# Dense layers without GpSimd: sums and low parts on VectorE, relu and squares on ScalarE, PSUM banks in pairs

## The chip, the cores and the metric

The kernel is one program on one core of a Trainium2 chip. The core has a matrix engine (TensorE, PE in the profile), a vector engine (VectorE, DVE), a scalar engine (ScalarE, ACT), a slower general engine (GpSimd, POOL) and SyncE (SP), which issues transfers. Each engine runs its own instructions in order and waits on semaphores for the others. The metric is the device time of one execution in microseconds (us).

## The reference, cut to what matters

Three layers follow each other over 8 batches of 576 tokens with 512 features.

```
x = linear attention of q, k, v                  # 8 heads of 64, out: 8 x 576 x 512
xk, xr = mu*x + (1-mu)*x_prev                    # two mixes with the token before
k = max(xk @ w_k, 0);  v = (k*k) @ w_v           # 512 -> 1024 -> 512
x2 = sigmoid(xr @ w_r) * v                       # 512 -> 512
gate = sigmoid(causal convolution of x2, 5 taps per feature)
out = (gate * (x2 @ w_val)) @ w_out              # two more 512 x 512
```

All matrices are fp32. The weights arrive as 64-bit bits and are turned into fp32 on the chip.

## The kernel before, in words

The first third of the time is attention (lines up to L760); beside it GpSimd, VectorE and ScalarE convert the weights. `moe()` then does the dense layers, one batch at a time: a loop of nine turns (`it`), in which turn `it` runs `prep` (the two mixes), `st_k`, `st_r` and `st_v` of batch `it`, and `conv`, `st_val` and `st_out` of batch `it-1`. On TensorE the stages of a turn stand in the order k, r, val, v, out. `x`, its mixes and `x2` have features on the partitions and 576 tokens (two halves of 288, `TB`) along the free dimension.

Each fp32 operand is split into a high part (a ScalarE copy to fp32r) and a low part (the operand less its high part); `product` adds three matmuls, high-high, high-low and low-high, into one PSUM bank. A matmul has 128x288 outputs. `st_k` and `st_v` use a scheme with seven products instead of eight: `combos` forms sums of the operand's quarters and `operand` splits them, into four buffers of the page `ops` (turn by turn); a product has 24 matmuls. `st_r`, `st_val` and `st_out` (`gemm`) have 96 plain matmuls each. That makes 7 x 24 x 2 + 3 x 96 = 624 matmuls in a full turn.

In the version before, the quarter sums of `combos` and many low parts (those not in `fast`) run on GpSimd through `pool_tt` (L395), in pieces of 288 columns; the rest of the low parts are VectorE's (`less`, L312). Results leave PSUM bank by bank, 288 columns at a time: copies by ScalarE, sums by VectorE (`dve`, L787), and relu with square in one VectorE instruction (`relu2`, L794). `fma` (L790) is VectorE's multiply by a per-feature factor and add, in `prep` and `conv`.

The pages are SBUF areas with changing contents. `xb` holds the batch's x with a zero column in front (its memset stands at L877, the load beside it in `prep`) and, later in the turn, x2 split for `st_val`. Weights of r, val, v and out come from DRAM in units of 1 MB into three buffers `u` (the first of v into `xf`); SyncE issues these loads and that of x in one queue.

`Order` plans all this when the program is built: each piece of work is an entry with an engine, a planned duration (`t_dve`, `t_act`, `t_pool`, `t_mm`), what it reads and writes, and a due time (`when`). `run` repeatedly takes the entry that could start first and appends its instructions to its engine, so that the durations in the plan decide the order on each engine. `Banks` gives out the eight PSUM banks. The waits between engines are then put in from the addresses that instructions touch.

Of the kernel before, what the change touches and what calls it, by code (L numbers as in the profile page):

```python
# [50 lines left out]
class Buf:  # L51


    def __init__(self, tag, make):
        self.tag, self.make, self.tile, self.users = tag, make, None, []
# [5 lines left out]
class Banks:  # L61


    def __init__(self, tiles, most):
        self.most, self.held, self.tiles = most, [], tiles

    def when(self, tasks, new):

        live, found, out = dict.fromkeys(self.most, 0), [], set(range(len(self.tiles)))
        for b in self.held:  # L70
            out.discard(b.place)
            ends = [tasks[u]["end"] for u in b.users]
            if None in ends:
                live[b.tag] += 1
            else:
                found.append((max(ends) + SEM, b.place, b))
# [4 lines left out]
        if any(b.tag in LAST for b in new) and sum(live[x] for x in LAST) >= len(self.tiles):  # L81
            return None
        found = sorted([(0.0, i, None) for i in out] + found, key=lambda f: f[:2])
        return found[:len(new)] if len(found) >= len(new) else None

    def take(self, found, new):
        for (_, place, old), b in zip(found, new):
            if old is not None:
                self.held.remove(old)
            b.place, b.tile = place, self.tiles[place]  # L90
            self.held.append(b)
# [12 lines left out]
class Order:  # L104
# [29 lines left out]
    def run(self):  # L134
# [10 lines left out]
        def ready(t):  # L145
            at = 0.0
            for d in t["deps"]:
# [3 lines left out]
                at = max(at, d["end"] + (SAME if d["eng"] == t["eng"] else SEM))  # L151
# [95 lines left out]
def build(ctx, tc, qt, kt, vv, wphi, mu, wk, wr, wv, wval, cw, wout, out):  # L247
# [5 lines left out]
    PSB = {"pj": 4, "qp": 2, "nm": 3, "kv": 2, "tb": 2, "mk": 8, "mo": 8}  # L253
# [24 lines left out]
    banks = [psum.tile([128, 512], F32, tag=f"b{i}", name=f"b{i}", bufs=1) for i in range(8)]  # L278
# [133 lines left out]
    def combine(quarters, n, emit):  # L412
# [16 lines left out]
        emit(1, s2, [t2])  # L429
        emit(2, a12, [t12])  # L430
# [53 lines left out]
    mut = const.tile([128, 2, 4], F32, name="mut")  # L484
    cwr = const.tile([128, 20, 2], I32, name="cwr")
# [257 lines left out]
    def moe():  # L743
# [41 lines left out]

        def dve(n, out, x, y, op, r, w):
            add("DVE", t_dve(n), lambda: tt(out=out(), in0=x(), in1=y(), op=op), r=r, w=w)  # L787

        def fma(n, out, x, scalar, y, r, w):
            add("DVE", t_dve(n) + 0.06, lambda: stt(out=out(), in0=x(), scalar=scalar(), in1=y(), op0=ALU.mult,  # L790
                                                    op1=ALU.add), r=r, w=w)

        def relu2(n, out, x, r, w):
            add("DVE", t_dve(n) + 0.06, lambda: stt(out=out(), in0=x(), scalar=0.0, in1=x(), op0=ALU.max,  # L794
                                                    op1=ALU.mult), r=r, w=w)

        def bank(o):
            return lambda: o[:, 0:TB]

        def product(o, stat, mov, first, last):  # L800

            k, n = 0, 3 * len(stat)
            for c, (wh, wl) in enumerate(stat):
                for a, b in ((wh, 0), (wh, 1), (wl, 0)):
                    mm(out=o[:, 0:TB], lhsT=a, rhs=mov[b][c], start=first and k == 0, stop=last and k == n - 1,  # L805
# [21 lines left out]
        def operand(x, fast):  # L827
# [3 lines left out]
            add("ACT", t_act(576), lambda: copy(h(F32R), x()), r=x.tok, w=h.tok)  # L831
# [6 lines left out]
        def combos(ops, qs, tmps, due, fast):  # L838

            each = list(enumerate(zip(qs, tmps)))  # L840

            def sub(p, i, out, x, y):
                due(p, i)
                pool_tt(576, out, x, y, ALU.subtract, tokens(x, y), out.tok)

            def op(p, k):
                for i, (q, tmp) in each:
                    due(p, i)
                    ops[p, i] = operand(tmp if k is None else q[k], p in fast)
# [3 lines left out]
            for i, (q, tmp) in each:  # L853
                sub(1 - 0.6, i, tmp, q[3], q[1])
                sub(1 - 0.4, i, q[1], q[1], q[0])
                sub(1 - 0.2, i, q[0], q[3], q[1])
            for p, k in enumerate((0, 2, 1, None, 3, 2), 1):
                op(p, k)
                if p == 2:
                    for i, (q, tmp) in each:  # L860
                        sub(2.2, i, q[2], q[0], q[2])
                yield

        def x2_at(it, m, h, n=TB):
            return At("x2", 2432 * (it % 2) + 608 * m + 32 + TB * h, n)

# [5 lines left out]
        def prep(it):  # L872
# [11 lines left out]
            for c in range(4):  # L884
                kh, cc = divmod(c, 2)
                when(it, -26 + 2.5 * c)
                dve(576, d[c], lambda c=c: x()[:, c, 1:577], lambda c=c: x()[:, c, 0:576], ALU.subtract,
                    x.tok + ["x0"], d[c].tok)
                fma(576, lambda kh=kh, cc=cc: view("xf", 1152 * kh, [128, 2, 2, 288])[:, :, cc],
# [275 lines left out]
```

## Time and profile before

| | us |
|---|---|
| median of 3 runs (1084.04 to 1088.51) | 1086.49 |
| profiled execution | 1086.6 |
| its span | 1084.8 |
| TensorE busy | 998.2 |
| VectorE busy | 891.2 |
| GpSimd busy | 686.1 |
| ScalarE busy | 495.0 |

The span is what the profile covers; 1.8 us of the profiled execution lie outside it. TensorE's instructions overlap (a weight load and the matmul before it, and each matmul with the next), so a busy TensorE need not be at its best rate; that rate is read as matmuls for each stretch of time. The chain of work that ended last is 50% TensorE, 29% VectorE and 11% GpSimd.

### The profile page before, as it was taken

How to read it: one execution, taken by the hardware profiler on the slowest of the kernel's cores; microseconds unless marked ns; L12 is line 12 of the kernel's file. 1: busy time of each engine (PE TensorE's matmuls, PEld its weight loads, DVE VectorE, ACT ScalarE, POOL GpSimd, SP SyncE). 2: the span in 40 equal slices, each digit the busy share in tenths (PEclk: the TensorE clock that was granted, in tenths of full speed). 3: DMA queues.
4: the chain of work that ended last, by engine and by line, in shares of the span. 5: the costliest groups of instructions: out<-in, count | busy, mean ns of one | idle time of the engine just before them, and what ended most of it. 6: DMA issues, size and time to landing. Idle time of an engine off the chain costs nothing.

```text
span 1084.8 us, 27608 instructions
## 1 busy us (share of the span) xinstructions
PE 998.2 (92%) x11456; PEld 957.2 (88%) x11456; DVE 891.2 (82%) x1328; ACT 495.0 (46%) x1031; POOL 686.1 (63%) x759
## 2 busy tenths in 40 slices
PE   8998898998988989998998899899889989988998
PEld 7888787887877988997998899899889989988998
DVE  6869686878878899789869959987995997799572
ACT  4676566766756343335342432523333252433342
POOL 1596887687745677486659548566864855686430
PEclk9999999999999998998999999899999989999999
DMA  7646567788844361483376157238516724841583
GB/s 207 192 145 190 162 207 236 235 273 252 264 148 143 134 239 40 140 303 111 117 267 209 40 190 268 95 117 282 194 40 206 276 72 138 291 164 53 181 276 123
DMA packets 93949, 195.86 MB, mean 181 GB/s; under 512 B 42496, under 2 KB 64384, under 8 KB 80512
## 3 DMA queue, kind: packets, MB, share of 16 engines
q1 hardware_dynamic: 84016, 184.00, 51.6%
q10 hardware_dynamic: 9808, 10.10, 2.7%
q8 instruction: 90, 1.47, 0.6%
q14 instruction: 35, 0.29, 0.1%
HBM read 161.57 MB, written 32.51 MB: 179 GB/s over the span
## 4 chain that ended last, share of the span: by engine, by line
PE 50%; DVE 29%; POOL 11%; issue 4%; ACT 3%; DMA 2%; SPq 1%; ACTq 0%; DVEq 0%; POOLq 0%
PE b L805 38%; DVE g L790 8%; PE b L649 4%; DVE ops L312 3%; DVE xb L790 3%; DVE x L787 3%; PE b L543 3%; DVE xf L790 2%; PE b L683 2%; DVE xb L787 2%; POOL xf L353 2%; DVE sp L787 2%; PE b L608 2%; POOL xb L395 1%; POOL xf L395 1%
## 5 line engine op out<-in xcount | busy, mean ns | idle before, releaser
L805 PE MATMUL b<-ops,wkt 128*128 128x288 f32 x1344 | 209.0, 318 | 38.2 <-DVE sp L787 15.4
L805 PEld LDWEIGHTS b<-ops,wkt 128*128 128x128 f32 x1344 | 198.7, 206 | 47.4 <-DVE sp L787 16.8
L805 PE MATMUL b<-y,u 128*128 128x288 f32 x1536 | 206.8, 295 | 1.7 <-DVE k L787 1.2
L805 PEld LDWEIGHTS b<-y,u 128*128 128x128 f32 x1536 | 204.4, 188 | 2.4 <-DVE k L787 1.4
L805 PE MATMUL b<-ops,u 128*128 128x288 f32 x1152 | 161.0, 297 | 8.7 <-POOL ops L395 5.3
L805 PEld LDWEIGHTS b<-ops,u 128*128 128x128 f32 x1152 | 154.7, 188 | 14.2 <-POOL ops L395 8.9
L790 DVE SCALAR_TENSOR_TENSOR g<-x,cwt,g 128x576 f32<-128x576 f32 x128 | 137.4, 1117 | 0.2
L395 POOL TENSOR_TENSOR ops<-xf,ops 128x288 fp32r<-128x288 f32 x84 | 91.4, 1109 | 54.6 <-ACT ops L309 47.7
L549 DVE TENSOR_REDUCE ot<-b 128x4 f32<-128x512 f32 (+1 forms) x160 | 94.3, 624 | 25.9 <-PE b L543 22.7
L309 ACT ACTIVATE ops<-k 128x576 fp32r<-128x576 f32 x96 | 66.1, 689 | 106.6 <-POOL k L395 59.2
L395 POOL TENSOR_TENSOR ops<-k,ops 128x288 fp32r<-128x288 f32 x56 | 54.5, 995 | 92.5 <-ACT ops L309 92.4
L312 DVE TENSOR_TENSOR ops<-k,ops 128x576 fp32r<-128x576 f32 x68 | 77.2, 1145 | 41.1 <-ACT ops L309 41.0
L395 POOL TENSOR_TENSOR k<-k 128x288 f32<-128x288 f32 x96 | 97.7, 1046 | 18.5 <-DVE ops L312 18.5
L805 PE MATMUL b<-xb,u 128*128 128x288 f32 x768 | 103.1, 295 | 0.0
L805 PEld LDWEIGHTS b<-xb,u 128*128 128x128 f32 x768 | 102.3, 188 | 0.0
L543 PE MATMUL b<-wph,ops 64*128 64x128 f32 x1152 | 80.6, 285 | 4.7 <-DVE k L551 1.2
L543 PEld LDWEIGHTS b<-wph,ops 64*128 64x128 f32 x1152 | 70.8, 191 | 12.9 <-issue 5.8
L794 DVE SCALAR_TENSOR_TENSOR k<-k 128x288 f32<-128x288 f32 x96 | 80.0, 852 | 2.0 <-POOL k L395 2.0
L683 PE MATMUL b<-g,y 128*64 128x65 f32 x2176 | 74.0, 224 | 6.2 <-ACT g L309 4.2
L683 PEld LDWEIGHTS b<-g,y 128*64 128x64 f32 x2176 | 68.1, 139 | 11.8 <-ACT g L309 4.8
L612 ACT ACTIVATE y<-b 128x512 f32<-128x512 f32 x128 | 68.8, 601 | 12.9 <-PE b L608 12.5
L395 POOL TENSOR_TENSOR xf<-xf 128x288 f32<-128x288 f32 (+1 forms) x62 | 67.5, 1112 | 5.2 <-DVE xf L364 5.1
(124 smaller groups left out, 1725.4 us busy)
## 6 DMA issues: line engine op xcount, KB each, us to landing
u<-ws SPq DMA_DIRECT2D x96, 1024.0 KB, 4.8
ws<-xb SPq DMA_DIRECT2D x24, 512.0 KB, 3.8
xs<-x SPq DMA_DIRECT2D x16, 576.0 KB, 4.5
xb<-xs SPq DMA_DIRECT2D x8, 1152.0 KB, 7.3
out<-ot ACTq DMA_DIRECT2D x64, 144.0 KB, 1.8
ops<-in_kt SPq DMA_DIRECT2D x15, 576.0 KB, 5.3
ops<-in_qt SPq DMA_DIRECT2D x15, 576.0 KB, 5.3
u<-in_vv SPq DMA_DIRECT2D x16, 512.0 KB, 5.5
```

The lines of the kernel that those rows point to most:

```text
L309: act(out=out, in_=x, func=AF.Copy)
L312: eng.tensor_tensor(out=out, in0=x, in1=hi.bitcast(F32), op=ALU.subtract)
L395: nc.gpsimd.tensor_tensor(out=o[:, c], in0=a[:, c], in1=b[:, c], op=op)
L543: mm(out=bs[ab][:, (at + i) * 128:(at + i + 1) * 128], lhsT=x[r, c:c + 128], rhs=wph[r], start=True, stop=True)
L549: add("DVE", t_dve(128 * n), lambda: nc.vector.tensor_reduce(out=m[:, 0:n, 0], in_=b3[:, 0:n], axis=AX.X, op=ALU.max, apply_absolute_value ...
L612: add("ACT", t_act(512), lambda half=half: act(out=e[:, ab, half, :], in_=b[:], func=AF.Exp, scale=-1.0 if half else 1.0), r=[b], w=[(e, a ...
L649: mm(out=b[y, o:o + 65], lhsT=lhs[:, y], rhs=vt[:, a:a + 65], start=(k == 0), stop=(c == 3), skip_group_check=True)
L683: mm(out=b[rows, at:at + 65], lhsT=lhs, rhs=a[:, o:o + 65], start=(k == 0), stop=(half == 1), skip_group_check=True)
L787: add("DVE", t_dve(n), lambda: tt(out=out(), in0=x(), in1=y(), op=op), r=r, w=w)
L790: add("DVE", t_dve(n) + 0.06, lambda: stt(out=out(), in0=x(), scalar=scalar(), in1=y(), op0=ALU.mult, op1=ALU.add), r=r, w=w)
L794: add("DVE", t_dve(n) + 0.06, lambda: stt(out=out(), in0=x(), scalar=0.0, in1=x(), op0=ALU.max, op1=ALU.mult), r=r, w=w)
L805: mm(out=o[:, 0:TB], lhsT=a, rhs=mov[b][c], start=first and k == 0, stop=last and k == n - 1, skip_group_check=True)
```

## The change

In `moe()` nothing runs on GpSimd any more. All low parts and all sums of quarters are VectorE's; those of `st_v` are single instructions over 1152 columns. Relu and square are two ScalarE instructions (`square`). The seven products are ordered so that running sums stay in PSUM (`PLAN`: product p adds into bank pair A, B or C, and only 0, 1 and 3 start afresh). PSUM is given out as four pairs of banks in the dense layers, and a result is read as 2 x 288 = 576 columns by one instruction. In `prep` the mix is a ScalarE scaling and one `fma` with 1-mu (`omm`) instead of a difference and an `fma`; the first tap of `conv` is a ScalarE scaling. The output leaves in 32 transfers of 288 KB instead of 64 of 144 KB. The planned durations become `d_time` and `a_time`, and an entry may follow another on TensorE without a planned gap. The diff, cut:

```
-    banks = [psum.tile([128, 512], F32, tag=f"b{i}", name=f"b{i}", bufs=1) for i in range(8)]
+    banks = [psum.tile([128, 2, 512], F32, tag=f"b{i}", name=f"b{i}", bufs=1) for i in range(4)]
...
-                at = max(at, d["end"] + (SAME if d["eng"] == t["eng"] else SEM))
+                at = max(at, d["end"] + (SEM if d["eng"] != t["eng"] else 0.0 if t["eng"] == "PE" else SAME))
...
+        def d_time(n):
+            return 0.15 + 0.00104 * n
+
+        def a_time(n):
+            return 0.13 + 0.00094 * n
...
-        def operand(x, fast):
+        def operand(x):
-            if fast:
-                add("DVE", t_dve(576), lambda: less(nc.vector, l(F32R), x(), h(F32R)), r=tokens(x, h), w=l.tok)
-            else:
-                pool_tt(576, lambda: l(F32R), x, h, ALU.subtract, tokens(x, h), l.tok)
+            add("DVE", d_time(576), lambda: less(nc.vector, l(F32R), x(), h(F32R)), r=tokens(x, h), w=l.tok)
...
-                pool_tt(576, out, x, y, ALU.subtract, tokens(x, y), out.tok)
+                dve(n, out, x, y, ALU.subtract, tokens(x, y), out.tok)
...
+                    acts(576, out, now, AF.Copy, x.tok + ["mut"], toks, scale=lambda r=r, c=c: mut[:, r, c:c + 1])
+                    fma(576, out, was, lambda r=r, c=c: omm[:, r, c:c + 1], out, x.tok + ["x0", "omm"], toks)
...
+        def square(it, t, x):
+            when(it, t)
+            acts(576, x, x, AF.Relu, [], x.tok)
+            acts(576, x, x, AF.Square, [], x.tok)
+
+        PLAN = ("A", "B", "A", "C", "A", "C", "A")
+        FRESH = (0, 1, 3)
...
+                    if p in (0, 2, 3, 4):
+                        d = (x11, None, x12, p5[m2], x22)[p]
+                        acts(576, d, b, AF.Copy, [o], d.tok)
+                        if p == 4:
+                            dve(576, x22, x22, p5[m2], ALU.add, p5[m2].tok, x22.tok)
+                            square(it, t + 4, x22)
+                    elif p == 6:
+                        acts(576, x21, b, AF.Relu, [o], x21.tok)
+                        acts(576, x21, x21, AF.Square, [], x21.tok)
                     else:
+                        d = x11 if p == 1 else x12
+                        dve(576, d, d, b, ALU.add, [o], d.tok)
+                        square(it, t + 4, d)
```

What the planner makes of it is seen in the order of the instructions. The first place is VectorE where `st_val` of a turn ends and `st_v` begins: `g` times the last results of val, the memset of the zero column of `xb` for the next batch, the low part of the last `y`, and low parts of v's operands (`ops` from `k`). Before:

```order
L787 TENSOR_TENSOR g<-g,b_80 128x288 [waits PE_49]
L787 TENSOR_TENSOR g<-g,b_84 128x288 [waits PE_49]
L877 MEMSET xb 128x4
L312 TENSOR_TENSOR y<-g,y 128x576 [waits Activation_49]
L312 TENSOR_TENSOR ops<-k_4936,ops 128x576 [waits Activation_49]
L787 TENSOR_TENSOR sp<-sp,b_86 128x288 [waits PE_49]
```

and now:

```order
L806 TENSOR_TENSOR g<-g,b_82 128x576 [waits PE_49]
L912 MEMSET xb 128x4 [waits DMAHW3_49]
L324 TENSOR_TENSOR y<-g,y 128x576 [waits Activation_49]
L324 TENSOR_TENSOR ops<-k_4934,ops 128x576 [waits Activation_49] x3
L806 TENSOR_TENSOR sp<-sp,b_83 128x576 [waits PE_49]
L324 TENSOR_TENSOR ops<-k_4934,ops 128x576 [waits Activation_49]
```

The memset stands at the same place, but now it waits for a transfer (DMAHW). The second place is SyncE's queue around that transfer, from the first unit of v (`xf`) to the load of x (`xb`). Before:

```order
L330 DMA xf<-ws 128x2048 [waits DVE_49,DMAHW2_49,Activation_49,Pool_49]
L330 DMA u_4938<-ws 128x2048 [waits DMAHW7_49,DMAHW3_49,PE_49]
L330 DMA u_4937<-ws 128x2048 [waits DMAHW4_49,PE_49]
L330 DMA u_4675<-ws 128x2048 [waits DMAHW5_49,DMAHW0_49,PE_49]
L330 DMA u_4938<-ws 128x2048 [waits DMAHW6_49,DMAHW3_49,PE_49]
L330 DMA xb<-xs_99 128x4x576 [waits DMAHW7_49,DMAHW1_49,DVE_49]
```

and now:

```order
L342 DMA xf<-ws 128x2048 [waits DVE_49]
L342 DMA u_4936<-ws 128x2048 [waits DMAHW1_49,PE_49]
L342 DMA u_4935<-ws 128x2048 [waits DMAHW3_49,DMAHW2_49,PE_49]
L342 DMA u_4673<-ws 128x2048 [waits DMAHW6_49,PE_49]
L342 DMA u_4936<-ws 128x2048 [waits DMAHW4_49,DMAHW1_49,PE_49]
L342 DMA xb<-xs_94 128x4x576 [waits DMAHW5_49,DVE_49]
```

The load of x stands at the same place, behind the unit whose buffer the last product of val frees. Before, the VectorE instruction that it waits for is the memset above; now it is an older one (a low part of `xb`), and the memset is the one that waits for the load. (The zero column and the loaded columns lie in one 4 x 577 area.) So it is for the loads of batches 2 to 7, six times. The third place is TensorE in `st_k` (`b_` are the banks, before eight single ones, now four pairs). Before:

```order
L805 MATMUL b_81<-ops,wkt 128x288 [waits DVE_49]
L805 MATMUL b_81<-ops,wkt 128x288 x5
L805 MATMUL b_82<-ops,wkt 128x288 [waits Activation_49]
L805 MATMUL b_82<-ops,wkt 128x288 [waits Pool_49]
L805 MATMUL b_82<-ops,wkt 128x288 x2
L805 MATMUL b_82<-ops,wkt 128x288 [waits Pool_49]
```

and now:

```order
L831 MATMUL b_82<-ops,wkt 128x288 [waits Activation_49]
L831 MATMUL b_82<-ops,wkt 128x288 [waits DVE_49]
L831 MATMUL b_82<-ops,wkt 128x288 x10
L831 MATMUL b_83<-ops,wkt 128x288 [waits Activation_49]
L831 MATMUL b_83<-ops,wkt 128x288 x11
```

Twelve matmuls now go to one pair, and what TensorE waits for is VectorE or ScalarE, where GpSimd stood before.

## Rows read from the trace of the kernel before

**Rows 1.** Windows by turn: PE, PEld, DVE, ACT, POOL busy; PEclk, DMA share, GB/s

```profile
345.20:511.35 166.15, 154.83 (x1094) 150.56 (x1093) 152.18 (x213) 63.19 (x124) 105.10 (x96) 0.96 0.48 165
511.35:604.43 93.08, 86.17 (x624) 84.42 (x624) 81.17 (x108) 34.95 (x70) 61.10 (x59) 0.98 0.50 173
604.43:699.04 94.61, 89.43 (x624) 87.31 (x624) 81.35 (x108) 34.64 (x69) 61.32 (x58) 0.95 0.49 170
...
980.08:1082.60 102.52, 101.13 (x744) 100.45 (x744) 66.02 (x106) 36.29 (x72) 37.21 (x40) 0.98 0.49 166
0.00:345.20 345.20, 305.71 (x6500) 279.31 (x6501) 266.61 (x475) 222.02 (x490) 237.39 (x333) 0.97 0.67 205
```

**Rows 2.** The same view in stretches of 20 us

```profile
540.00:560.00 20.00, 20.00 (x153) 20.00 (x152) 10.65 (x19) 7.52 (x13) 7.68 (x9) 1.00 0.65 235
...
1040.00:1060.00 20.00, 20.00 (x153) 19.99 (x151) 19.93 (x31) 7.19 (x16) 2.13 (x3) 1.00 0.79 266
```

**Rows 3.** The chain that ended last: start us, length us, what

```profile
601.93 2.08 DVE y L312 x3
604.43 44.81 PE b L805 x324
```

**Rows 4.** TensorE's timeline there: start, length, what [idle before, releaser]

```profile
591.64 9.18 PE L805 MATMUL b<-ops,wkt 128*128 128x288 f32 x54 [2.08 <-ACT ot L309]
604.43 1.88 PE L805 MATMUL b<-ops,wkt 128*128 128x288 f32 x9 [3.61 <-DVE sp L787]
```

**Rows 5.** Windows of 0.5 us, TensorE alone: busy, clock, DMA share, GB/s

```profile
591.50:592.00 0.50, 0.36 (x1) 0.60 0.00 0
...
594.50:595.00 0.50, 0.50 (x2) 0.50 0.62 210
595.00:595.50 0.50, 0.50 (x6) 0.99 0.50 182
```

**Rows 6.** VectorE's groups by form from 530 us: busy us, mean ns, idle

```profile
L790 DVE SCALAR_TENSOR_TENSOR g<-x,cwt,g 128x576 f32<-128x576 f32 x96 | 102.9, 1121 | 0.2
...
L312 DVE TENSOR_TENSOR ops<-k,ops 128x576 fp32r<-128x576 f32 x47 | 57.3, 1230 | 37.5 <-ACT ops L309 37.5
...
L787 DVE TENSOR_TENSOR sp<-sp,b 128x288 f32<-128x288 f32 x68 | 28.0, 443 | 3.2 <-PE b L805 3.2
```

**Rows 7.** The same for 1043 us to the end, where GpSimd is idle

```profile
L790 DVE SCALAR_TENSOR_TENSOR g<-x,cwt,g 128x576 f32<-128x576 f32 x15 | 11.7, 811 | 0.1
...
L312 DVE TENSOR_TENSOR xb<-x,xb 128x576 fp32r<-128x576 f32 x4 | 3.0, 746 | 0.0
...
L787 DVE TENSOR_TENSOR x<-x,sp 128x288 f32<-128x288 f32 x2 | 0.8, 449 | 0.0
L787 DVE TENSOR_TENSOR sp<-sp,b 128x288 f32<-128x288 f32 x2 | 0.8, 446 | 0.0
```

**Rows 8.** ScalarE's groups by form: two from 530 us on, one of attention

```profile
L309 ACT ACTIVATE ops<-k 128x576 fp32r<-128x576 f32 x70 | 48.3, 690 | 86.1 <-POOL k L395 50.2 <-PE b L805 34.2 <-POOL ops L395 0.9
...
L309 ACT ACTIVATE ot<-b 128x288 f32<-128x288 f32 x56 | 22.8, 407 | 47.5 <-PE b L805 41.8 <-ACT ot L309 4.7 <-DMA out<-ot 1.0
...
L612 ACT ACTIVATE y<-b 128x512 f32<-128x512 f32 x128 | 68.8, 601 | 12.9 <-PE b L608 12.5 <-DVE k L551 0.2
```

**Rows 9.** Timelines of TensorE, VectorE and SyncE where v of a turn starts

```profile
549.68 3.36 PE L805 MATMUL b<-ops,xf 128*128 128x288 f32 x24
...
550.29 0.06 DVE L877 MEMSET xb<- 128x4 f32 x1
...
550.43 0.37 SPq L330 DMA_DIRECT2D xb<-xs  x1
```

**Rows 10.** Transfers from 535 to 562 us: KB each, us from issue to landing

```profile
xb<-xs SPq DMA_DIRECT2D x1, 1152.0 KB, 7.3
```

**Rows 11.** Line L877: what its engine idled for before it (us, times)

```profile
  DMA xb<-xs: 3.9, 1
```

**Rows 12.** GpSimd's timeline, sums of quarters for k of the first turn

```profile
333.30 7.69 POOL L395 TENSOR_TENSOR xf<-xf 128x288 f32<-128x288 f32 x6
```

More of the change, by code (lines that the diff above doesn't have):

```diff
@@ L54, in __init__ @@
     def __init__(self, tag, make):
-        self.tag, self.make, self.tile, self.users = tag, make, None, []
+        self.tag, self.make, self.tile, self.users, self.wide = tag, make, None, [], False
     def __getitem__(self, i):
@@ L75, in when @@
             else:
-                found.append((max(ends) + SEM, b.place, b))
+                found += [(max(ends) + SEM, k, b) for k in b.places]
         for b in new:
@@ L80, in when @@
                 return None
-        if any(b.tag in LAST for b in new) and sum(live[x] for x in LAST) >= len(self.tiles):
+        if any(b.tag in LAST for b in new) and sum(live[x] for x in LAST) >= 2 * len(self.pairs):
             return None
         found = sorted([(0.0, i, None) for i in out] + found, key=lambda f: f[:2])
+        if new[0].wide:
+            at = {f[1]: f for f in found}
+            two = [(max(at[k][0], at[k + 1][0]), k) for k in range(0, 2 * len(self.pairs), 2) if k in at and k + 1 in at]
+            if not two:
+                return None
+            t, k = min(two)
+            return [(t, k, at[k][2]), (t, k + 1, at[k + 1][2])]
         return found[:len(new)] if len(found) >= len(new) else None
     def take(self, found, new):
[L87 to L90, printed above, removed]
+        for old in {id(f[2]): f[2] for f in found if f[2] is not None}.values():
+            self.held.remove(old)
+        if new[0].wide:
+            b = new[0]
+            b.places, b.tile = [f[1] for f in found], self.pairs[found[0][1] // 2]
+            self.held.append(b)
+            return
+        for (_, place, _), b in zip(found, new):
+            b.places, b.tile = [place], self.pairs[place // 2][:, place % 2]
             self.held.append(b)
@@ L784, in tokens, with acts, go, wide @@
             return [t for x in xs for t in x.tok]
+        def d_time(n):
+            return 0.15 + 0.00104 * n
+        def a_time(n):
+            return 0.13 + 0.00094 * n
         def dve(n, out, x, y, op, r, w):
-            add("DVE", t_dve(n), lambda: tt(out=out(), in0=x(), in1=y(), op=op), r=r, w=w)
+            add("DVE", d_time(n), lambda: tt(out=out(), in0=x(), in1=y(), op=op), r=r, w=w)
         def fma(n, out, x, scalar, y, r, w):
[L790 to L800, printed above, removed]
+            add("DVE", d_time(n) + 0.06, lambda: stt(out=out(), in0=x(), scalar=scalar(), in1=y(), op0=ALU.mult,
+                                                     op1=ALU.add), r=r, w=w)
+        def acts(n, out, x, func, r, w, **kw):
+            def go():
+                more = {k: v() for k, v in kw.items()}
+                act(out=out(), in_=x(), func=func, **more)
+            add("ACT", a_time(n), go, r=r, w=w)
+        def wide():
+            b = ps("mk")
+            b.wide = True
+            return b
+        def both(o):
+            return lambda: o[:, :, 0:TB]
+        def product(o, half, stat, mov, first, last):
             k, n = 0, 3 * len(stat)
@@ L804, in product @@
                 for a, b in ((wh, 0), (wh, 1), (wl, 0)):
-                    mm(out=o[:, 0:TB], lhsT=a, rhs=mov[b][c], start=first and k == 0, stop=last and k == n - 1,
+                    mm(out=o[:, half, 0:TB], lhsT=a, rhs=mov[b][c], start=first and k == 0, stop=last and k == n - 1,
                        skip_group_check=True)
@@ L957, in st_v @@
+            s, p5, u2 = (At("sp", 576 * i, 2, 288) for i in range(3))
             banks = {}
@@ L1047, in st_out, with after @@
         def st_out(i, it, t0):
-            def after(m, h, o, b, t):
-                d = At("ot", 288 * (next(turn_out) % 3), 288)
-                add("ACT", t_act(TB), lambda: copy(d(), b()), r=[o], w=d.tok)
-                load(lambda: out[m * 128:(m + 1) * 128, i * S + h * TB:i * S + h * TB + TB], lambda: d(), 147456,
-                     r=d.tok, by="ACT")
+            def after(m, o, b, t):
+                d = At("ot", 576 * (next(turn_out) % 2), 576)
+                acts(576, lambda: halves(d()), b, AF.Copy, [o], d.tok)
+                load(lambda: out[m * 128:(m + 1) * 128, i * S:i * S + S], lambda: d(), 294912, r=d.tok, by="ACT")
             gemm("wout", it, t0, "y", after)
```

220 lines of the change are left out of this document (103 added, 117 removed), and 4 rows, old and new, of the table PAGES.

## The prediction

> **What bounds the kernel now.** I read the windows by turn first, then the chain of waits, then TensorE's timeline at the place where the chain leaves it, and last the groups of VectorE and ScalarE by form.
>
> Where nothing holds it, TensorE does 153 of the dense layers' matmuls in 20 us [rows 2], 0.1307 us each. A turn's 624 matmuls would take 81.6 us. They take 93.1 or 94.6 [rows 1]; from 511.35 to 980.08 five turns take 468.73 us, 93.75 each, so each loses 12.2. The first stretch (345.20 to 511.35, 1094 matmuls, 143.0 at the full rate) loses 23.1, and the last (744 matmuls, 97.2) loses 5.3. Of the 89 us lost, about 84 lie ahead of the last stretch.
>
> The reader is to see who takes them. VectorE is busy 81 us of a turn and GpSimd 61 [rows 1]. The chain runs through VectorE until the low parts of `y`, then through 324 matmuls without a break [rows 3]: st_k's results and st_r's operand come too late. In that place TensorE waits 2.08 us for a ScalarE copy and 3.61 for a VectorE sum [rows 4]. After the first wait its granted clock is at the half level (0.5, 1.2 GHz) from about 591.5 to 595.0 [rows 5], which costs another 1.7 us. VectorE is the limit of this stretch, and it is slow: with GpSimd at work an instruction with two SBUF inputs of 576 columns takes 1.12 to 1.23 us [rows 6], near the end, with GpSimd idle, 0.811 and 0.746 [rows 7].
>
> **The change, part by part.**
>
> *VectorE.* In a full turn it had 108 instructions and 81 us. Counting the code of the changed kernel: 43 two-input instructions of 576 SBUF columns (12 in splits of y and xb, 7 low parts, 4 sums and 2 adds in k, 14 low parts and 4 adds or gates in v), 4 sums of 1152, 24 `fma` (8 in prep, 16 in conv) and 11 that read 576 columns of PSUM. Alone they cost 0.75, about 1.34, 0.811 and about 0.74 us. The second is an estimate: 576 columns take 0.746 and 288 take 0.449 [rows 7], 1.03 ns a column, so 1152 take 0.746 + 0.594. The fourth likewise, 0.446 + 0.297. Sum: 32.3 + 5.4 + 19.5 + 8.1 = 65.3 us, 80% of TensorE's 81.6. The far end, all at the prices beside GpSimd (1.23, 2.46, 1.121): 52.9 + 9.8 + 26.9 + 8.1 = 97.7. I take the near end, because in the dense layers GpSimd has nothing left, and rows 7 are the same instructions with GpSimd idle.
>
> PSUM readers took 0.443 beside GpSimd [rows 6] and 0.446 without it [rows 7]. The Trainium skill, "GPSIMD Engine Reference", section "Key points", says that GpSimd shares its SBUF interfaces with VectorE and contends with VectorE instructions that have two SBUF inputs; by that rule nothing is to be had from those eleven, and these rows agree. By it the sum is the 65.3 above, and a sum in which everything got quicker in proportion (81 x 0.746/1.23) would be wrong.
>
> *ScalarE.* It gains the scalings, the relu and the squares: 85 instructions a turn, 63 from SBUF and 22 from PSUM. One of 576 columns costs 0.69 from SBUF, and about 0.656 from PSUM (0.601 for 512 and 0.407 for 288 columns, 0.87 ns a column) [rows 8]. Sum 43.5 + 14.4 = 57.9 us, 71% of a turn. Twelve of them have a factor per partition, which no row shows. Only the Trainium skill has a price, "ScalarE: Activation LUTs", section "What ACT_TABLE_LOAD costs": about 93 ns for each such operand, so 1.1 us more a turn, and ScalarE would be at 59.0 of 81.6; the sum below stays.
>
> *The turns.* With VectorE at 65 and ScalarE at 58, TensorE is the bound. The tightest stretch is v's end to k's end, when TensorE does out and k (264 matmuls, 34.5 us): by the order VectorE has 42 instructions there, 32.5 us, ScalarE 53, 36 us. Both end about with TensorE, but what k and r need stands early in it: the last operand of k is VectorE's 32nd, the last part of `y` its 28th. So these waits go, and with them the half clock. I leave 1 us a turn for handovers; 0 and 5 are its ends (5: ScalarE 1.5 late and its waits on VectorE in line). Five turns: -60.9 + 5 = -55.9.
>
> *The first turns.* The 23.1 us go likewise, but turn 0 has no val between k and v to cover the squares: 5 of them stay (0 to 10). -18.1.
>
> *The first operands.* GpSimd formed the sums for the first k in pieces, 7.7 us for six [rows 12]; VectorE needs 3 x 0.75 to 1.23 for them. Up to 5.4 us, down to nothing if attention's end holds TensorE; I take 3. -3.
>
> *The wait that is added.* The memset of the zero column now waits for the load of x. Before, the load waited for it. In the row at v's start [rows 9] v begins at 549.68, the memset runs at 550.29 and the load is issued at 550.43, 0.75 after v's start; it lands 7.3 later [rows 10]. Nothing in the change brings it forward, since it stands behind the unit that val's last product frees. So VectorE stands still until 8.05 after v's start, with the last `y` and three low parts of v's operands queued behind the memset. TensorE has four split operands then, two products, 48 matmuls, 6.3 us. The next low part ends at 8.05 + 0.06 + 0.75 + 0.75, near 9.65. TensorE waits 3.35 us. Once in the old trace VectorE did wait for this load, 3.9 us [rows 11]. The wait of 2.08 cost 1.7 more by the clock. A turn's mean clock is 0.98 or 0.95 [rows 1]: one stretch of 3.4 us at half takes 0.5 x 3.4 / 93 = 0.018 of it, so a turn with two long waits has one to three such stretches, others none. I take 1.2 for each wait (0 to 1.7). 4.55 each, six times: +27.3. The ends: nothing, if the load came in 4 us; 30, if each wait costs the clock.
>
> *The end.* The last stretch keeps its 5.3. The last copy is 576 columns instead of 288, 0.656 for 0.407, and its transfer twice as large: +0.5.
>
> *Attention* is planned anew, but its work is the same; I put it at 0, with 8 either way.
>
> **Sum**, against the profiled execution's own 1086.6 (span 1084.8 and 1.8 around it; the median of the runs shown is 1086.49, the same): 1086.6 - 55.9 - 18.1 - 3 + 27.3 + 0.5 = 1037.4 us.
>
> **The rivals.**
>
> *The memset's wait is hidden.* If x lands sooner, or v's operands are further ahead than the four buffers, TensorE never sees it: 1037 - 27 = 1010. For it: DMA was at 0.65 of its time there [rows 2]. Against it: four buffers, and 7.3 us.
>
> *VectorE and ScalarE hand over too often.* Most low parts need a ScalarE copy first, and both queues are in order; ScalarE has 36 us of work in a stretch of 34.5. If each turn loses 5 us more there, seven turns make 35: 1072. For it: VectorE idled 37.5 us ahead of 47 such low parts, for ScalarE [rows 6]. Against it: what TensorE needs is placed early.
>
> *The change doesn't do what it says: two-input instructions stay slow without GpSimd.* Then VectorE has 97.7 us a turn, 4 more than the 93.75 of today, seven times: 1115, slower. It decides from a mean price of about 1.17 us on. Against it rows 7; for it, that these are few and from the end, when DMA and TensorE are calmer.
>
> *Four pairs are too few banks.* A pair is free only when all its 576 columns are read. If TensorE had to wait for each of the 33 results of a turn, 0.656 and a handover of 0.2, that is 28 us a turn, 1264 in all (eight turns); slower than before from 6.5 us a turn on. Against it: in k a pair is written again only after another product, some 4 us after its results stand.
>
> **How the numbers follow.** Forecast 0.60; the wait hidden 0.16; handovers 0.17; slow instructions 0.03; too few banks 0.04. The range goes from the second case to the third: 1008 to 1074, which takes in 8 us for attention about the forecast. Within 0.5% (5.4 us, about what a measurement of this kernel can tell from no change) lie 0.02 of the handovers and 0.01 each of the last two; slower 0.01, 0.02 and 0.03. Faster 0.90, same 0.04, slower 0.06.
>
> **What would show it.** GpSimd without an instruction after attention; `fma` on 576 columns at 0.81 us and low parts at 0.75 in all turns; VectorE busy 65 us a turn, ScalarE 58; a turn of some 87 us; the waits for `sp` and `ot` inside k gone. The memset's row with six waits of about 7 us for the load of x, and TensorE waiting 3 to 4 us for low parts of v right behind two products. Wrong it would be if v runs through without that wait (then 1010), if TensorE waits inside k for operands or banks, or if the low parts are still above 1 us.

## The result and the profile after

The changed kernel takes 1073.2 us (median of 7 runs, 1068.55 to 1080.89), the kernel before 1086.23 (7 runs beside it, 1083.49 to 1088.51). The ratio is 0.9891, with a 95% interval of 0.9859 to 0.9923: 1.1% faster. The forecast was 1037. The profiled execution has a span of 1071.4 (before 1084.8).

The windows of the changed kernel, with columns as in [rows 1]. The first window ends where TensorE has done attention's last transposes and the dense products run on alone; 30 of their matmuls are done by then. In the kernel before the same point, 36 dense matmuls done, is 345.20.

```profile
0.00:380.43 380.43, 318.81 (x6494) 286.78 (x6495) 261.56 (x472) 228.88 (x494) 222.86 (x326) 0.96 0.62 186
380.43:488.19 107.76, 107.76 (x813) 107.55 (x812) 77.25 (x106) 74.03 (x123) 0.00 (x0) 1.00 0.47 162
488.19:575.51 87.32, 84.54 (x625) 84.31 (x624) 60.60 (x83) 52.21 (x86) 0.00 (x0) 0.98 0.54 184
575.51:661.81 86.30, 83.02 (x625) 82.78 (x624) 60.46 (x83) 52.22 (x86) 0.00 (x0) 1.00 0.54 186
749.18:838.50 89.32, 85.76 (x625) 85.49 (x624) 60.71 (x83) 52.89 (x86) 0.00 (x0) 0.96 0.54 183
924.94:1071.40 146.46, 139.12 (x1032) 138.41 (x1031) 94.80 (x129) 74.43 (x119) 0.00 (x0) 0.99 0.54 184
```

Two things stand in it. A turn takes 86.3 to 89.3 us instead of 93.1 to 94.6, with GpSimd idle and VectorE at 60.6 instead of 81 us. And the first window, attention, has the same matmuls as the last row of [rows 1], but for six dense ones (0.8 us), and lasts 380.4 us instead of 345.2. The dense part shrank from 1084.8 - 345.2 = 739.6 to 1071.4 - 380.4 = 691.0 us, by 48.6; attention grew by 35.2; the difference of 13.4 is what is left.

The groups of VectorE and ScalarE by form, from 400 to 1000 us (busy us, mean ns | idle before):

```profile
L809 DVE SCALAR_TENSOR_TENSOR g<-x,cwt,g 128x576 f32<-128x576 f32 x112 | 87.9, 811 | 0.1
L324 DVE TENSOR_TENSOR ops<-k,ops 128x576 fp32r<-128x576 f32 x86 | 62.5, 752 | 3.3 <-ACT ops L815 3.2
L806 DVE TENSOR_TENSOR k<-k 128x1152 f32<-128x1152 f32 x24 | 32.5, 1355 | 0.5
...
L806 DVE TENSOR_TENSOR g<-g,b 128x576 f32<-128x576 f32 x26 | 19.6, 754 | 52.1 <-PE b L831 52.1
...
L815 ACT ACTIVATE k<-k 128x576 f32<-128x576 f32 x101 | 63.4, 679 | 0.0
...
L815 ACT ACTIVATE xf<-xb,mut 128x576 f32<-128x576 f32 x28 | 21.4, 764 | 0.0
```

These are the prices of [rows 7] in all turns: `fma` 0.811 us where [rows 6] have 1.121, low parts 0.752 for 1.230. The factor per partition costs ScalarE 764 - 679 = 85 ns.

The timelines of SyncE, VectorE and TensorE where a turn's v starts (start us, length us; v's first product begins at 481.54), which answers to [rows 9]:

```profile
482.10 0.43 SPq L342 DMA_DIRECT2D xb<-xs  x1
...
481.74 0.75 DVE L806 TENSOR_TENSOR g<-g,b 128x576 f32<-128x576 f32 x1 [0.92 <-PE b L831]
489.53 0.75 DVE L324 TENSOR_TENSOR y<-g,y 128x576 fp32r<-128x576 f32 x1 [7.04 <-ACT ops L815]
489.55 0.06 DVE L912 MEMSET xb<- 128x4 f32 x1
490.19 2.09 DVE L324 TENSOR_TENSOR ops<-k,ops 128x576 fp32r<-128x576 f32 x3
...
484.73 3.49 PE L831 MATMUL b<-ops,u 128*128 128x288 f32 x25
491.00 9.25 PE L831 MATMUL b<-ops,u 128*128 128x288 f32 x56 [2.78 <-DVE ops L324]
```

VectorE stands for 7.04 us until the load of x, issued at 482.10, has landed 7.4 later; then the memset and, behind it, the last `y` and three low parts follow. The row names a ScalarE copy of an operand as the releaser, but the copy that `y` itself needs had ended at 483.27; the load is what came last. TensorE waits 2.78 us behind two products. The windows right behind it show the clock (busy, clock, DMA share, GB/s at the end of each row):

```profile
491.00:493.00 2.00, 2.00 (x11) 2.00 (x12) 2.00 (x4) 0.00 (x0) 0.00 (x0) 0.74 0.63 254
493.00:495.00 2.00, 2.00 (x11) 2.00 (x10) 2.00 (x4) 1.35 (x2) 0.00 (x0) 0.50 0.00 0
495.00:497.00 2.00, 2.00 (x15) 2.00 (x15) 1.07 (x2) 1.11 (x2) 0.00 (x0) 0.90 0.27 45
```

And the sum of TensorE's waits from 376 us to the end (us in total, times, longest; two waits of 0.4 us for `y` are all the rest):

```profile
PE b L831 <- DVE ops L324: 17.5, 6, 3.3
```

Attention, up to 330 us, has waits that the kernel before hardly has. VectorE's reduce of one PSUM result (`ot`, L562) waits for ScalarE's exponentials of another result (`y`, L625), and ScalarE for VectorE:

```profile
DVE ot L562 <- PE b L556: 30.5, 19, 7.2
DVE ot L562 <- ACT y L625: 13.2, 6, 5.7
...
ACT y L625 <- DVE ot L562: 7.4, 6, 2.8
```

In the kernel before, up to 345 us, the same three are 22.7, 2.0 and none.

### The profile page after: what moved, and what is told of

Read it like the earlier page. It is cut to its first block, busy times and chain, and to the rows that moved or that the text cites. A ratio compares the mean times of both kernels' runs of the same rounds, so it can differ in the third digit from the quotient of the medians.

```text
span 1071.4 us, 26797 instructions
## 1 busy us (share of the span) xinstructions
PE 987.8 (92%) x11456; PEld 953.7 (89%) x11456; DVE 736.7 (69%) x1121; ACT 638.3 (60%) x1159; POOL 222.9 (21%) x326
## 4 chain that ended last, share of the span: by engine, by line
PE 76%; DVE 9%; ACT 5%; POOL 4%; issue 4%; DMA 1%; SPq 0%; ACTq 0%; POOLq 0%; DVEq 0%
PE b L831 63%; PE b L556 4%; PE b L696 3%; PE b L662 3%; DVE ot L562 3%; DVE k L564 2%; DVE sp L564 1%; PE b L621 1%; ACT y L625 1%; POOL xf L365 1%; ACT u L608 1%; PE b L736 1%; POOL xb L407 1%; ACT x L321 1%; POOL ot L718 1%
## 5 line engine op out<-in xcount | busy, mean ns | idle before, releaser
L831 PE MATMUL b<-ops,u 128*128 128x288 f32 x1152 | 165.0, 306 | 17.5 <-DVE ops L324 17.5
L831 PEld LDWEIGHTS b<-ops,u 128*128 128x128 f32 x1152 | 162.7, 198 | 18.9 <-DVE ops L324 18.9
L831 PE MATMUL b<-ops,wkt 128*128 128x288 f32 x1344 | 179.4, 294 | 0.0
L831 PEld LDWEIGHTS b<-ops,wkt 128*128 128x128 f32 x1344 | 178.2, 188 | 0.1
L562 DVE TENSOR_REDUCE ot<-b 128x4 f32<-128x512 f32 (+1 forms) x160 | 95.4, 626 | 56.1 <-PE b L556 36.1
L809 DVE SCALAR_TENSOR_TENSOR g<-x,cwt,g 128x576 f32<-128x576 f32 x128 | 100.3, 811 | 1.0 <-ACT g L815 0.8
L556 PE MATMUL b<-wph,ops 64*128 64x128 f32 x1152 | 88.9, 296 | 11.1 <-ACT y L625 4.8
L625 ACT ACTIVATE y<-b 128x512 f32<-128x512 f32 x128 | 71.0, 598 | 44.4 <-PE b L556 13.2
L815 ACT ACTIVATE y<-g 128x576 fp32r<-128x576 f32 x32 | 22.0, 686 | 84.8 <-DVE g L806 84.8
L815 ACT ACTIVATE k<-k 128x576 f32<-128x576 f32 x112 | 70.4, 679 | 0.1
L324 DVE TENSOR_TENSOR y<-g,y 128x576 fp32r<-128x576 f32 x32 | 24.2, 757 | 62.7 <-ACT ops L815 35.5
L806 DVE TENSOR_TENSOR g<-g,b 128x576 f32<-128x576 f32 x32 | 24.1, 754 | 57.8 <-PE b L831 57.8
L321 ACT ACTIVATE x<-b 128x260 f32<-128x260 f32 (+3 forms) x96 | 39.6, 423 | 33.9 <-PE b L696 7.2
```

The costliest lines, as they stand in the source:

```text
L321: act(out=out, in_=x, func=AF.Copy)
L324: eng.tensor_tensor(out=out, in0=x, in1=hi.bitcast(F32), op=ALU.subtract)
L556: mm(out=bs[ab][:, (at + i) * 128:(at + i + 1) * 128], lhsT=x[r, c:c + 128], rhs=wph[r], start=True, stop=True)
L562: add("DVE", t_dve(128 * n), lambda: nc.vector.tensor_reduce(out=m[:, 0:n, 0], in_=b3[:, 0:n], axis=AX.X, op=ALU.max, apply_absolute_value ...
L625: add("ACT", t_act(512), lambda half=half: act(out=e[:, ab, half, :], in_=b[:], func=AF.Exp, scale=-1.0 if half else 1.0), r=[b], w=[(e, a ...
L806: add("DVE", d_time(n), lambda: tt(out=out(), in0=x(), in1=y(), op=op), r=r, w=w)
```

## The experiments

Two theories stood for attention. PAIRS: the waits are put in per PSUM tile, not per address, so that in pair tiles work on one bank waits for work on its neighbour. PLAN: `combine` emits the weights' combinations in another order, and the planner then orders the second half of attention differently (TensorE's rows are the same up to the 1639th).

**before_pairs.** Only the banks, in the kernel before:

```
-    banks = [psum.tile([128, 512], ...) for i in range(8)]
+    twos = [psum.tile([128, 2, 512], ...) for i in range(4)]
+    banks = [twos[i // 2][:, i % 2] for i in range(8)]
```

> The kernel before, with its eight PSUM banks cut out of four pair tiles and nothing else changed; every engine's instructions stand in the same order as before. Theory PAIRS (attention lost 31 us because the waits are put in per PSUM tile, so that work on one half of a pair waits for work on the other half): the continuous dense matmuls start at 365 to 380 us instead of 345, and the time is 1105 to 1120 us. Theory PLAN (attention lost them because the weights' combinations are emitted in another order, which reorders the second half of attention): start at 345, time 1086 within 5.

Measured: 1178.29 us, ratio 1.0832 (1.0803 to 1.0861).

```profile
0.00:376.69 376.69, 312.77 (x6500) 281.00 (x6501) 269.99 (x475) 225.93 (x490) 235.07 (x333) 0.98 0.62 188
376.69:1175.00 798.31, 706.35 (x4959) 686.47 (x4957) 614.41 (x853) 277.31 (x541) 439.16 (x426) 0.95 0.46 157
```

Attention takes 376.7 instead of 345.2: +31.5 from the tiles alone, with every engine's order unchanged. The dense part takes 798.3 instead of 739.6, since there too the old code uses the halves apart; that part was not expected. What the tile does is seen in the program's waits. ScalarE's first exponentials in the kernel before, then with pairs (the brackets name the engines whose semaphore the instruction waits for):

```
8 L612 ACTIVATE y<-b_80 128x512 [waits PE_49]
16 L625 ACTIVATE y<-b_80 128x256 [waits PE_49]

8 L613 ACTIVATE y<-b_80 128x512 [waits DVE_49,PE_49]
16 L626 ACTIVATE y<-b_80 128x256 [waits DVE_49]
```

The added wait is for a VectorE subtraction that reads columns 512 to 1023 of the same pair, while this one reads 0 to 511: two readers of different banks in a row. On ScalarE 102 instructions got such a wait for VectorE that they had not. So the sentence in the description above, that waits come from the addresses that instructions touch, does not hold for PSUM: there the tile counts.

**before_swap.** Only the emission, in the kernel before:

```
-        emit(1, s2, [t2])
-        emit(2, a12, [t12])
+        emit(1, a12, [t12])
+        emit(2, s2, [t2])
```

> The kernel before, with only the emission of the second and third weight combination swapped in `combine`, as the change has it (the two sets of weights then stand in each other's place, so the output isn't the reference's). The order in attention is then that of the changed kernel from TensorE's 1640th instruction on. Theory PLAN: dense matmuls start near 376, time near 1117. Theory PAIRS: start at 345 within 5, time 1086 within 6.

Measured: 1085.96 us, ratio 0.9992 (0.9976 to 1.0008). The dense matmuls run on alone from 345.80:

```profile
345.80 17.84 PE L805 MATMUL b<-ops,wkt 128*128 128x288 f32 x132
```

PLAN falls: on single banks the other order by itself costs nothing.

**after_ones.** The changed kernel, with single banks until the first pair is asked for:

```
+    ones = psum("ones")
+    banks = [[ones.tile([128, 512], ...) for h in range(2)] for i in range(4)]
+    def joined():
+        pools.close()
+        twos = psum("twos")
+        return [twos.tile([128, 2, 512], ...) for i in range(4)]
...
+        if new[0].wide and isinstance(self.pairs[0], list) and any(live.values()):
+            return None
...
+            if isinstance(self.pairs[i], list):
+                self.pairs = self.joined()
```

> The changed kernel, in which attention has eight tiles of one bank, and the four pair tiles are made when the first dense product is planned; the order in attention is unchanged. Theory PAIRS: dense matmuls start at 345 to 355 instead of 376, time 1042 to 1055. Theory PLAN: start at 376, time 1073 within 4.

Measured: 1031.83 us, ratio to the kernel before 0.9496 (0.9459 to 0.9532), so 41.4 us less than the changed kernel.

```profile
0.00:337.64 337.64, 298.38 (x6495) 272.57 (x6495) 260.54 (x472) 225.44 (x494) 225.06 (x326) 0.99 0.69 210
```

Attention is back at 337.6, below the 345.2 of before and the 345 to 355 that were expected; the dense part keeps 1028.1 - 337.6 = 690.5 (691.0 in the changed kernel). The reduces of `ot` wait 18.7 us for TensorE, where they waited 30.5.

Both directions agree: pairs put in cost 31.5 us of attention, pairs taken out give 42.8, and in neither case does any engine's order change. The granted clock in this window is 0.99, in the changed kernel's 0.96, so up to some 12 of the 42.8 us went with the clock; before_pairs has 0.98 against 0.97, and its 31.5 us owe nothing to it.

**after_noswap.** The changed kernel with the old emission.

> The changed kernel with the weights' combinations emitted in the old order (the second and third sets of weights then stand in each other's place, so the output isn't the reference's). Attention's order is then that of the kernel before, on pair tiles. If the new order costs something only where pairs add waits, the first dense product starts at 361 to 367 us (363.9 in the kernel before with pairs) instead of 375.8, and the time is near 1062. If the order costs nothing: 376 and 1073.

Measured: 1064.36 us, one run, and the dense matmuls alone from 373.94:

```profile
373.94 18.50 PE L831 MATMUL b<-ops,wkt 128*128 128x288 f32 x138
```

That is 6.5 us before the changed kernel's 380.4. It is inconclusive: after_zero, below, has almost the changed kernel's order in attention and needs 386.2, after_ones and best share almost the same one and need 337.6 and 342.1, so attention varies by some 5 us between executions, and this was a single execution. Its time lies below all seven of the changed kernel, though (1068.55 the fastest), so that the new order may cost something on pairs stays open.

**after_zero.** The load of x reads what the memset writes:

```
-                 r=[("xs", it, c) for c in range(2)], w=x.tok)
+                 r=[("xs", it, c) for c in range(2)] + ["x0"], w=x.tok)
```

> The changed kernel, in which the load of x waits for the memset of the zero column, so that VectorE no longer waits for the load. Theory WAIT (TensorE's six stalls at v's third product come from that wait: 17.5 us of waiting, and the clock after it): 18 to 30 us less, 1043 to 1055, and the six waits of about 3 us ahead of v's products are gone. Rival SERIES (v's operands are late anyway, since VectorE works them off in line with the gates; the wait only takes the blame): at most 8 us less, 1065 to 1073, TensorE still waits there.

Measured: 1047.68 us, ratio 0.9624 (0.9591 to 0.9658): 25.5 us less than the changed kernel. The windows, and TensorE and VectorE at the same place (v starts at 487.28):

```profile
0.00:386.18 386.18, 323.32 (x6495) 291.10 (x6495) 260.44 (x468) 227.16 (x491) 221.80 (x326) 0.95 0.60 183
386.18:1049.60 663.42, 658.91 (x4965) 658.23 (x4962) 481.28 (x653) 410.83 (x669) 0.00 (x0) 1.00 0.55 188
```

```profile
490.47 9.76 PE L831 MATMUL b<-ops,u 128*128 128x288 f32 x72
...
488.19 0.06 DVE L912 MEMSET xb<- 128x4 f32 x1
489.04 0.76 DVE L324 TENSOR_TENSOR y<-g,y 128x576 fp32r<-128x576 f32 x1 [0.80 <-ACT y L815]
489.85 0.76 DVE L324 TENSOR_TENSOR ops<-k,ops 128x576 fp32r<-128x576 f32 x1
```

The memset runs 0.9 us after v's start, the next low part ends 3.3 us after v's start, and three products follow without a break. From 381 us on TensorE waits 0.8 us in all. The dense part falls from 691.0 to 663.4. WAIT holds, SERIES falls. (The planner moves a few other instructions along, 22 of VectorE's 1121.) Of the 27.6 us, 17.5 were TensorE's waits; the other 10 are the half clock behind them (11 matmuls in 2 us above, where 15 fit): in the changed kernel the granted clocks of the five turns and the last stretch, 0.98, 1.00, 0.98, 0.96, 0.98 and 0.99, come to 10 us of lost time.

**best.** Both repairs together.

> The changed kernel with both repairs: attention on eight tiles of one bank, and the load of x behind the memset. If the two losses are separate, as they lie in different stretches, the gains add: 1073.2 - 41.4 - 25.5 = 1006, between 1003 and 1011. Rival: they overlap (with attention done earlier the dense layers run into something else), 1015 or more.

Measured: 1006.54 us, ratio 0.9271 (0.9257 to 0.9285). The two add as they should. This is the version that beats both. Its windows, then all that TensorE waits for from 340 us on:

```profile
0.00:342.10 342.10, 304.48 (x6495) 278.63 (x6495) 258.09 (x468) 223.41 (x491) 225.11 (x326) 0.97 0.67 207
450.00:531.60 81.60, 81.60 (x618) 81.60 (x617) 60.22 (x82) 51.97 (x85) 0.00 (x0) 1.00 0.56 191
```

```profile
PE p L849 <- ACT y L833: 0.4, 1, 0.4
PE p L849 <- DVE y L342: 0.4, 1, 0.4
```

TensorE is never idle in 81.6 us of a turn, at full clock. The dense part takes 1005.5 - 342.1 = 663.4.

**best_gpsimd, gpsimd_two, gpsimd_one.** Useless work on GpSimd beside each low part, all into one scratch tile, in the kernel best:

```
+    for i in range(8):                      # best_gpsimd
+        nc.gpsimd.tensor_tensor(out=junk, in0=hi[:, j:j + 96], in1=hi[:, j + 288:j + 384], op=ALU.add)
...
+    nc.gpsimd.tensor_tensor(out=junk, in0=hi[:, 0:96], in1=ident[:, 0:96], op=ALU.add)     # the other two
+    for _ in range(3):                      # gpsimd_two
+        nc.gpsimd.tensor_tensor(out=junk, in0=ident[:, 0:96], in1=ident[:, 32:128], op=ALU.add)
+    for _ in range(4):                      # gpsimd_one
+        nc.gpsimd.tensor_scalar(out=junk, in0=ident[:, 0:96], scalar1=LEAST, scalar2=MOST, op0=ALU.max, op1=ALU.min)
...
-        for _ in range(8):                  # gpsimd_one, in warm()
+        for _ in range(4):
```

The last two lines halve the idle matmuls with which TensorE starts the program in gpsimd_one; they lie far ahead of the stretch that is read here.

> The kernel with both repairs, in which GpSimd does useless work in the dense layers: for each operand eight sums of 96 columns of its high part into a scratch tile that nobody reads, some 50 us a turn. Theory SHARED (VectorE's two-input instructions were slow before because GpSimd was at work beside them): fma goes from 0.81 towards 1.12 us, low parts from 0.75 to 1.1 or more, instructions that read PSUM stay at 0.75; VectorE is busy 85 to 95 us a turn, and the time is 1050 to 1110. Rival OTHER (they were slow because of DMA traffic or TensorE): fma and low parts within 5% of before, time within 6 us of the kernel without that work.

> The kernel with both repairs and useless work on GpSimd as in the run best_gpsimd, but less and apart: for each operand one sum that reads it, and three sums of 96 columns of a constant tile, into a scratch tile; some 2.3 us an operand, 48 us a turn, and hardly anyone waits for GpSimd. Theory SHARED: VectorE's instructions with two SBUF inputs are slower (fma 0.88 to 0.95, low parts 0.80 to 0.87), those that read PSUM stay at 0.75; VectorE is then busy 70 to 75 us of 81.6, still not the bound, and the time is at most 15 us above that kernel's 1006. Rival OTHER: fma at 0.81 and low parts at 0.755 as without that work, time within 4.

> As gpsimd_two, but with four GpSimd instructions with a single SBUF input (limits of 96 columns of the constant tile) in place of the three sums. If it is GpSimd's work as such that slows VectorE, fma and low parts are slower here too, by as much for each us that GpSimd is busy. If it is the two inputs on both sides, they stay near 0.82 and 0.76 but for the one sum in five.

Measured: 1231.11 us (ratio 1.1352, 1.1323 to 1.1382), 1021.95 (0.9399, 0.9364 to 0.9433) and 1043.54 (0.9598, 0.957 to 0.9626). The first time says nothing of the theories: GpSimd fell behind and became the bound, and ScalarE waited for it before it could write an operand anew:

```profile
ACT ops L834 <- POOL junk L883: 353.2, 123, 5.0
```

In the other two ScalarE still waited 58.2 and 103.5 us in this way, against the expectation, so their times are no prices of the contention either. The durations are. From 400 to 980 us in gpsimd_two:

```profile
L828 DVE SCALAR_TENSOR_TENSOR g<-x,cwt,g 128x576 f32<-128x576 f32 x117 | 106.7, 935 | 1.2 <-ACT g L834 1.2
L342 DVE TENSOR_TENSOR ops<-k,ops 128x576 fp32r<-128x576 f32 x84 | 73.7, 888 | 20.0 <-ACT ops L834 18.6
...
L825 DVE TENSOR_TENSOR g<-g,p 128x576 f32<-128x576 f32 x28 | 21.1, 754 | 32.8 <-PE p L850 32.8
```

and in gpsimd_one, with GpSimd's own two rows behind:

```profile
L828 DVE SCALAR_TENSOR_TENSOR g<-x,cwt,g 128x576 f32<-128x576 f32 x112 | 90.5, 830 | 1.2 <-ACT g L834 0.8
L342 DVE TENSOR_TENSOR ops<-k,ops 128x576 fp32r<-128x576 f32 x79 | 62.8, 807 | 38.1 <-ACT ops L834 37.6
...
L882 POOL TENSOR_SCALAR junk<-ident 128x96 f32<-128x96 f32 x570 | 391.2, 686 | 47.8
L880 POOL TENSOR_TENSOR junk<-ops,ident 128x96 f32<-128x96 f32 x142 | 75.5, 532 | 66.1 <-ACT ops L834 55.3
```

SHARED holds in its direction: with two-input work on GpSimd the low parts go from 0.755 to 0.888 us and `fma` from 0.815 to 0.935, while readers of PSUM stay at 0.754. With one-input work, although GpSimd is busy longer (467 of 580 us against 425), they only reach 0.807 and 0.830. The Trainium skill, "GPSIMD Engine Reference", section "Key points", names VectorE's two SBUF inputs as a condition; the rows agree. They add that GpSimd's own instruction matters too; whether by its number of inputs or by what else sets a limit apart from a sum, they do not show.

The size that SHARED expected of best_gpsimd did not come: with GpSimd busy 529 of 600 us, `fma` took 0.941 us and low parts 0.832, not 1.1 and more. The durations of single `fma` instructions from 400 to 980 us (shortest, median and longest in ns) say why, first in the kernel before, then in gpsimd_two and gpsimd_one:

```profile
L790 DVE SCALAR_TENSOR_TENSOR g<-x,cwt,g x112: 804/1351/1392, 405.1 to 976.4; 128x576 f32<-128x576 f32 x112
L828 DVE SCALAR_TENSOR_TENSOR g<-x,cwt,g x117: 803/945/1014, 401.1 to 979.8; 128x576 f32<-128x576 f32 x117
L828 DVE SCALAR_TENSOR_TENSOR g<-x,cwt,g x112: 802/812/949, 405.8 to 947.9; 128x576 f32<-128x576 f32 x112
```

Beside GpSimd's pieces of 288 columns the median is 0.55 us above the shortest, beside its sums of 96 columns 0.14, beside one-input work 0.01. Useless work in small pieces could therefore not bring back the prices of [rows 6]. In the kernel before itself they go with GpSimd: of its 160 `fma` in this stretch, the 33 with GpSimd idle beside them took 0.806 us on average, the 97 wholly beside its work 1.29.

**best_lowparts.** 13 of a turn's 21 low parts of `operand` back on GpSimd:

```
+            if fast:
                 add("DVE", d_time(576), lambda: less(nc.vector, l(F32R), x(), h(F32R)), r=tokens(x, h), w=l.tok)
+            else:
+                pool_tt(576, lambda: l(F32R), x, h, ALU.subtract, tokens(x, h), l.tok)
```

> The kernel with both repairs, with 13 of a full turn's 21 low parts of seven-product operands back on GpSimd in pieces of 288 columns, as in the kernel before. VectorE then has some 10 us less of a turn, but its other two-input instructions overlap GpSimd's 17 us. If VectorE's share is all that counts, nothing changes (within 4 us), since TensorE is the bound. If the length of the way from an operand to its low part counts (GpSimd 1.3 to 1.5 us against 0.75), TensorE waits again for operands: 10 to 30 us slower.

Measured: 1016.47 us, ratio 0.9368 (0.9347 to 0.9388), 9.9 us slower than best, by size almost the second answer's 10. One piece of 288 columns takes GpSimd 1.0 to 1.2 us, so a low part takes 2.0 to 2.5, not 1.3 to 1.5, against VectorE's 0.755:

```profile
L425 POOL TENSOR_TENSOR ops<-xf,ops 128x288 fp32r<-128x288 f32 x76 | 92.4, 1239 | 30.6 <-ACT ops L833 30.5
```

But it is not for these low parts that TensorE waits. Beside two waits of 0.4 us it waits five times, for VectorE's adds of results in PSUM (`k`). The sum, then the place of the longest wait:

```profile
PE p L849 <- DVE k L824: 5.1, 5, 2.6
...
397.26 7.77 DVE L827 SCALAR_TENSOR_TENSOR g<-x,cwt,g 128x576 f32<-128x576 f32 x6
404.95 0.74 DVE L824 TENSOR_TENSOR k<-k,p 128x576 f32<-128x576 f32 x1
...
405.75 2.53 PE L849 MATMUL p<-ops,wkt 128*128 128x288 f32 x9 [2.59 <-DVE k L824]
```

Six `fma` ahead of the add took 7.77 us with GpSimd at work nearly all the while; at 0.815 each they take 4.9. Two of the shorter waits, at 573.86 and 657.69, have `fma` and low parts of 1.36 us ahead of the add in the same way. By the trace, then, the mechanism is neither of the two that were expected: it is the slower VectorE beside GpSimd, in front of an add that TensorE needs. With the half clock behind the longest wait this accounts for most of the 8.2 us by which the dense part grew (671.6 for 663.4); the rest was not taken apart.

**best_gap.** The planned gap between dependent entries of TensorE put back into best:

```
-                at = max(at, d["end"] + (SEM if d["eng"] != t["eng"] else 0.0 if t["eng"] == "PE" else SAME))
+                at = max(at, d["end"] + (SAME if d["eng"] == t["eng"] else SEM))
```

> The kernel with both repairs, with the planned gap of 0.13 us between dependent entries of TensorE put back; the order on VectorE and ScalarE then differs from the second product of the dense layers on. The prediction gave this part of the change no term: 1006 within 5. Rival: the plan without gap keeps VectorE's order nearer to what TensorE does, and with it TensorE waits again; 10 us or more slower.

Measured: 1048.76 us, ratio 0.9656 (0.9628 to 0.9683), 42.2 us slower than best; the rival holds. The dense part has 1046.2 - 339.4 = 706.8 instead of 663.4, and TensorE waits for ScalarE to read banks (`sp`):

```profile
PE p L849 <- ACT sp L833: 26.5, 16, 2.7
```

The gap is a number in the plan only; no instruction changes but its place. On TensorE too the order is another: it now takes two products of v in turn, six matmuls at a time.

```profile
444.57 0.96 PE L849 MATMUL p<-ops,xf 128*128 128x288 f32 x6
445.36 0.96 PE L849 MATMUL p<-ops,u 128*128 128x288 f32 x6
```

And ScalarE has four scalings of the next x (between 454.07 and 457.43) ahead of the copy at 457.90 in the same v. Which of the two the 42 us come from was not taken apart.

## Why the prediction missed

The step that failed is the one that read "*Attention* is planned anew, but its work is the same; I put it at 0, with 8 either way". It should have been +38: the 35.2 of the table below, and the 3 that were expected off it. In its place the runs showed pair tiles: 31.5 us of attention from them alone in before_pairs, and attention back at 337.6 without them in after_ones. The working under it was incomplete in two ways. A new order ("planned anew") was taken for the only risk; before_swap shows that on single banks it was harmless. And a rival on pairs was weighed, but for the dense layers alone ("A pair is free only when all its 576 columns are read"), where a pair is used as a whole and TensorE waits for no bank. Attention uses the halves apart, and there the pair binds two results together that have nothing to do with each other. The rows of before could not show this; the waits of the changed program could, had they been compared in attention as they were in the dense layers.

Point by point, from the profiles:

| term | predicted | measured |
|---|---|---|
| dense turns, first turns and end, without the new wait | -73.5 | 663.4 (after_zero, best) - 739.6 = -76.2 |
| the memset's wait | +27.3 | 691.0 - 663.4 = +27.6 (25.5 by the medians) |
| attention and first operands without pairs | -3 (-13 to +8) | 337.6 or 342.1 - 345.2 = -7.6 or -3.1 |
| attention's pair tiles | none | 380.4 - 345.2 = +35.2 with the first operands in it |

The measured terms give 1086.6 - 76.2 + 27.6 + 35.2 = 1073.2. That they meet the time is no check, since they are differences of the same stretches; the check is that after_ones, after_zero and best each take their term away.

*Prices.* `fma` 0.81 and low parts 0.75 came out, and so did the PSUM readers (0.754 for an estimated 0.74) and 1152 columns (1.355 for 1.34). VectorE's 60.6 us a turn lie below the 65.3 because consecutive instructions overlap in the record: three low parts take 2.09 us, not 2.26. ScalarE shows 52.2 for 57.9 for the same reason. Its factor per partition costs 85 ns, where the prediction has 93.

*The wait.* The load takes 7.4 us, VectorE stands until 8.0 us after v's start (8.05 predicted), TensorE waits 2.78 to 3.3 us (3.35), six times, right behind two products. One wait costs 4.6 us with its clock; 4.55 was taken. That the two agree so well is luck: the wait itself is 2.9 us on average, not 3.35, and the clock behind it costs 1.7, not 1.2.

*Rivals.* "Hand over too often" gave 1072 and so nearly the time, and it set the end of the range next to which the time lies. That is luck too: in best TensorE waits 0.8 us in the whole dense part. "The wait is hidden" falls by after_zero, "slow instructions" by the prices. "Too few banks" falls where it was placed. (Its price to be slower than before is 49.2 / 8 = 6.2 us a turn, not 6.5. And the instructions of [rows 7] were no calmer case: those shown lie between 1043 and 1060 us, where [rows 2] have DMA at 0.79 and TensorE without a break.)

*What the forecast did not list.* The zero gap in the plan is worth 42 us (best_gap); it went without a term only because the order was read from the changed program, which has it.

## What to carry to other kernels

Before banks are joined into one tile, list who uses the parts: a stage that uses them singly takes over its neighbour's waits, those of mere readers included. Compare the waits of the whole program before and after, stage by stage, also where the change means to do nothing; the order alone does not show them. A clearing write beside a load into the same page cost nothing here where the load waited for it; where it waited for the load, VectorE stood still for most of the transfer (7.04 of 7.4 us).

## What the runs showed of the hardware

Beside GpSimd's two-input sums, VectorE's `fma` (two SBUF inputs, 576 columns) took a step longer, and the step went with the size of GpSimd's pieces: a median of 1.351 us beside 288 columns, 0.945 beside 96, against 0.815 with GpSimd idle. GpSimd's one-input instructions slowed it little (median 0.812; low parts 0.755 to 0.807 on average, with GpSimd at work 80% of the time, 13% in two-input sums); two-input sums of 96 columns at 73% brought low parts to 0.888.

A TensorE wait of 2.8 us was followed by 6 us with a granted clock of 0.74, 0.50 and 0.90 in turn; over six such waits that raised the price of one from 2.9 us (17.5 / 6) to 4.6 on average. It is an average only: the longest wait, 3.3 us at 578.82, lies in the turn with a granted clock of 1.00, and the turn from 749.18, with a wait of 2.9, has 0.96. All of this is from single profiles.
